# Attention scores from block-diagonal float32 query tiles of 64 queries, and a new table of priorities, in an attention and two-layer kernel on one core

## The chip, the core and the metric

The kernel runs on one core of one Trainium2 chip. The metric is device time in microseconds (us) for one execution. A core has five engines with instruction queues of their own, each worked off in order: PE (TensorE, matrix products), DVE (VectorE), ACT (ScalarE), POOL (GpSimd) and SP (SyncE, which here issues every DMA). The weight loads of PE have a row of their own, PEld. Sixteen DMA engines carry out the transfers that SP issues.

## The reference

There are four batches, eight heads, 576 positions and 64 elements to a head. Attention is causal by blocks of 64 positions: a query sees all keys of its own block and of the blocks before it. Two layers with 2048 hidden units follow on the 2304 x 512 result.

```python
batch, n_heads, seq, head_dim = (4, 8, 576, 64)
scores = scale * np.matmul(q, k.transpose(0, 1, 3, 2))
mask = pos[:, None] // 64 >= pos[None, :] // 64
scores = np.where(mask, scores, -1000000000.0)
attn = np.exp(scores - np.max(scores, axis=-1, keepdims=True))
attn = attn / (np.sum(attn, axis=-1, keepdims=True) + 1e-09)
x = np.matmul(attn, v)                 # then heads side by side: 2304 x 512
h = x @ w_in;  g = np.maximum(h, 0) + alpha * np.minimum(h, 0);  x = g @ w_out
h = x @ w_in2; g = h / (1 + np.exp(-1.702 * h));                 out = g @ w_out2
```

Weights of the layers come as float64 bits and are narrowed in the kernel.

## The kernel before

**Passes.** A pass handles one pair of heads of one batch. Batch 0 is cut into eight half passes, first queries 0 to 319 of the four pairs (group 0), then queries 320 to 575 (group 1); the other three batches are twelve whole passes.

**One pass.** SP loads q, k and v of the pair in rows of one position (256 bytes), q twice, so that it stands twice side by side (`load`). PE transposes them (`prep_t`, tile `tp`). `prep_out` splits the float32 values into a high fp32r part (ACT) and the rest (DVE): of k, the high part lies on 64 partitions and the rest on the other 64; of q there are two tiles, high and rest. `score` multiplies the five query tiles of `QT` (64, 128, 128, 128 and 128 queries against 64, 192, 320, 448 and 576 keys), for each head alone, high q and then rest q against the k tile. A tile of 128 queries holds two blocks, so for the first of them the last 64 keys are overwritten with a large number (the memset in `soft`) before the row minimum (DVE) and the exponential with its sum (ACT). `high` writes the normalized weights as float16 (ACT), `rest` what is missing to it (DVE), into the tile `hl` of one head. A DMA transpose then turns each `hl` of 12 (group 0) or 18 (group 1) chunks of 128 columns into `pt`, of which there are two buffers. `pv` multiplies `pt` with v, which is held as three bf16 parts, and `pv_out` stores the result to `xs`.

**Around it.** While attention runs, PE also computes a first part of layer 0 (the block products, lines 206 and 250 to 252, tiles `h` and `x`), 384 products of 288 columns for each batch, as soon as that batch's attention is done. `warm` products fill PE at the start. After the last pass the pools are swapped, and the rest of both layers follows (lines 744 and 819).

**Order.** Each step is entered with `at(kind, n, fn)`. Its priority is n + 0.1 ORDER + SHIFT of its kind; `arrange` then fixes an order for each engine with its own costs and writes it into the program. `SHIFT` is a table of numbers for each kind of step.

Of the kernel before, what the change touches and what calls it, by code (L numbers as in the profile page):

```python
# [23 lines left out]
QT = [(0, 64, 64, 1, 0), (64, 128, 192, 2, 2), (192, 128, 320, 3, 6), (320, 128, 448, 4, 0), (448, 128, 576, 5, 8)]  # L24

GRP = [((0, 1, 2), 0, 320, 12), ((3, 4), 320, 256, 18)]


PV = [[
    [(0, 64, 0, 0, (0,)), (64, 256, 0, 0, (1, 2)), (128, 64, 1, 64, (1,)), (192, 128, 1, 0, (2,)), (256, 64, 2, 64, (2,))],  # L30
    [(0, 256, 0, 0, (3, 4)), (0, 256, 1, 0, (3, 4)), (0, 256, 2, 0, (3, 4)), (64, 64, 3, 64, (3,)), (128, 128, 3, 0, (4,)),
     (192, 64, 4, 64, (4,))],
], [
    [(0, 64, 0, 0, (0,)), (64, 256, 0, 0, (1, 2)), (64, 256, 1, 0, (1, 2)), (192, 128, 2, 0, (2,))],
    [(0, 256, 0, 0, (3, 4)), (0, 256, 1, 0, (3, 4)), (0, 256, 2, 0, (3, 4)), (0, 256, 3, 0, (3, 4)), (128, 128, 4, 0, (4,))],
]]

SLOT = [((0, 1), (2,)), ((3,), (4,))]
# [10 lines left out]
    "comb 2": 35.0, "comb 3": -62.2, "first": 58.5, "gate": -35.3, "gate 2": 49.1, "gemm1": 46.5,  # L49
    "gemm1 2": 12.5, "gemm2": 59.1, "half": 110.6, "half out": -22.5, "high": 19.0, "load alpha": -0.4,  # L50
    "load k": 9.7, "load q": -168.0, "load v": -25.2, "load w": 61.9, "load w 2": 11.9, "load w 3": 3.0,
    "load wc": -24.2, "load x": -20.5, "narrow": 297.4, "narrow 2": 65.6, "narrow 3": 20.9, "norm": 13.4,
    "out": 4.8, "prep out": 20.2, "prep t": -7.1, "prep v": 81.6, "pv": 5.9, "pv out": 23.1, "rest": 20.2,
    "score": -5.4, "second": 58.6, "setup": -9.8, "snap": -57.0, "soft": -4.0, "split g": 64.1,
    "split g 2": -56.1, "split w": -8.4, "split w 2": 13.3, "split w 3": -3.0, "split x": 56.6,
    "split x 2": 192.1, "sums": -166.0, "warm": 67.8,
# [5 lines left out]
def kernel(  # L62
# [208 lines left out]
    def plan_x(i, n_split):  # L271
# [7 lines left out]
        for c in range(KD):  # L279
# [11 lines left out]
    nat = {"q": one.tile([128, 9, 2, D], F32, name="nat_q"), "k": one.tile([128, 10, D], F32, name="nat_k"),  # L291
           "v": one.tile([128, 9, D], F32, name="nat_v")}
    vp = [one.tile([128, 9, 4, D], BF16, name=f"vp{i}") for i in range(2)]
    hl = [[one.tile([128, 128 * g[3]], F16, name=f"hl{j}{x}") for x in range(NHL[j])] for j, g in enumerate(GRP)]
    stats = [one.tile([128, 3, 6], F32, name=f"stat{j}") for j in range(4)]

    def hl_part(j, x, m, n, h):
        o = 128 * (QT[j][4] + x * QT[j][3])
        return hl[0 if j < 3 else 1][h][0:m, o + 64 * h:o + 64 * h + n]


    def setup():
        pool.memset(ident, 0.0)
        pool.affine_select(out=ident, in_=ident, pattern=[[-1, 128]], compare_op=ALU.not_equal,
                           fill=1.0, base=0, channel_multiplier=1)
        pool.memset(mk_l, 0.0)
        pool.memset(nat["k"][:, 9], 0.0)
        for t in vp:
            pool.memset(t[:, :, 3], 0.0)
        for t in hl[0] + hl[1]:  # L310
            dve.memset(t, 0.0)
        for t in stats:
            pool.memset(t, 1.0)
# [7 lines left out]
    def load(i, nm):  # L321
        b, p, gs = passes[i]
        src = {"q": q, "k": k, "v": v}[nm][b, 2 * p:2 * p + 2].rearrange("h t d -> (h t) d").rearrange("(c p) d -> p c d", p=128)
        if nm == "q":
            c = slice(0, 9) if len(gs) == 2 else (slice(0, 7), slice(2, 9))[gs[0]]
            for y in range(2):
                sp.dma_start(out=nat["q"][:, c, y], in_=src[:, c])
        elif nm == "v" or gs[0] == 0:
            c = slice(0, 9 if nm == "k" or gs[-1] == 1 else 7)
            sp.dma_start(out=nat[nm][:, c], in_=src[:, c])  # L330


    CH = ((0, 1, 2, 3), (4, 5, 6, 7)), ((0, 1, 2), (4, 5, 6)), ((2, 3, 4), (7, 8))

    def chunks(i, what):
        gs = passes[i][2]
        return CH[0 if len(gs) == 2 else 1 + gs[0]][int(what[1])]

    def prep_t(i, what):
        ps = ps_a.tile([128, 512], F32, tag="tv", bufs=2, name="tp")  # L340
        st["tp", i, what] = ps
        if what == "k":

            ts = [nat["k"][:, c:c + 2] for c in range(0, 8, 2)]
        elif what == "tail":
            ts = [nat["k"][:, 8:10]] + [nat["q"][:, 8]] * (len(passes[i][2]) == 2)
        else:
            ts = [nat["q"][:, c] for c in chunks(i, what)]
        for z, t in enumerate(ts):
            pe.transpose(ps[:, 128 * z:128 * z + 128], t.rearrange("p c d -> p (c d)"), ident)  # L350

    def prep_out(i, what):


        ps = st.pop(("tp", i, what))
        gs = passes[i][2]
        if what in ("k", "tail"):
            if i < N0:

                p = passes[i][1]  # L360
                if what == "k" and p == 0:
                    st["k0"] = blk.tile([128, KD, S], F32R, tag="xl0", name="k0")
                if what == "k":
                    st["k0", p] = st["k0"][:, 2 * p:2 * p + 2] if p < KD // 2 else two.tile([128, 2, S], F32R, tag="k", name="k0")
                z = st["k0", p]
            else:
                if what == "k":
                    st[i, "k"] = two.tile([128, 2, S], F32R, tag="k", name="ks")
                z = st[i, "k"]
            z = z.rearrange("p h t -> p (h t)").rearrange("p (c t) -> p c t", t=128)  # L370
            half = [slice(0, 64), slice(64, 128)]
            y = ps.rearrange("p (c t) -> p c t", t=128)
            if what == "k":
                kinds = [(x, y[half[x]], slice(x, 8, 2)) for x in range(2)]
            else:
                kinds = [(0, y[half[0], 0:1], slice(8, 9))]
# [4 lines left out]
        if what == "k" or what == "tail" and len(gs) == 1:  # L381
            return
        if (i, "q") not in st:
            st[i, "q"] = two.tile([128, 2, 2 * S], F32R, tag="q", name="qs")
        if what == "tail":
            c0, y = 8, ps[:, 128:256]
        else:
            cs = chunks(i, what)
            c0, y = cs[0], ps[:, 0:128 * len(cs)]
        t = slice(128 * c0, 128 * c0 + y.shape[-1])  # L390
        z = st[i, "q"]
        hi_part(z[:, 0, t], y, -scale)
# [12 lines left out]
    for i, (b, p, gs) in enumerate(passes):  # L405
        first.append(2 * len(slots))
        for g in gs:
            for s in range(2):
                slots.append((i, g, s))
# [735 lines left out]
```

## Time and profile before

| | |
|---|---|
| median of 3 runs | 1064.5 us (1062.02 to 1065.96) |
| profiled execution | 1065.77 us |
| its span, first to last instruction | 1064.0 us |
| PE, DVE, ACT, POOL busy | 994.3, 739.2, 614.7, 368.0 us |
| mean granted clock of PE | 0.980 of full |
| DMA | 308081 packets, 216.92 MB |

The profiled execution is one of the program on the chip. Its span leaves 1.77 us outside. Busy times are sums over one engine's instructions in the span; engines work beside one another, so they don't add up to it. The ends of matrix products are modelled, so PE counts as busy for a little longer than it takes columns in.

### The profile page before, as it was taken

To read this page: it belongs to the slowest core of one execution; us is meant where nothing else is said; L and a number is where in the kernel's file an instruction comes from. 1 tells how busy PE (TensorE), PEld (TensorE's weight loads), DVE (VectorE), ACT (ScalarE), POOL (GpSimd) and SP (SyncE) were. 2 spreads that over 40 slices of the span, in tenths; PEclk is the share of its full clock that TensorE was granted. 3 is DMA by queue.
4 is the path that set the end of the run, shared out by engine and by line. 5 is a ranking of instruction groups with operands and counts; after the bars stand their busy time and mean duration, and the time that the engine had idled before them with its cause. 6 is when DMAs were issued, how large, how long until landed. Compare 5 with 4: busy or idle time off the path is not lost.

```text
span 1064.0 us, 19650 instructions
## 1 busy us (share of the span) xinstructions
PE 994.3 (93%) x6934; PEld 892.6 (84%) x6934; DVE 739.2 (69%) x1434; ACT 614.7 (58%) x1492; POOL 368.0 (35%) x385
## 2 busy tenths in 40 slices
PE   6776888999999999899999998989999999999998
PEld 4454778889888989899989897878888999999897
DVE  7868998898988985768886877778843544443422
ACT  6777888988888984455554545445542443342332
POOL 3334352535242442665453543423331311111100
PEclk8889899999999999999999999999999999999999
DMA  7999989998999977675556487988675666574360
GB/s 185 190 195 201 210 175 222 212 221 196 220 207 217 207 164 194 225 254 175 194 178 218 159 288 239 317 273 270 226 241 165 233 194 195 176 243 130 119 198 30
DMA packets 308081, 216.92 MB, mean 204 GB/s; under 512 B 219664, under 2 KB 246288, under 8 KB 307984
## 3 DMA queue, kind: packets, MB, share of 16 engines
q1 hardware_dynamic: 307984, 215.67, 74.4%
q8 instruction: 55, 0.90, 0.4%
q14 instruction: 42, 0.34, 0.1%
HBM read 143.27 MB, written 40.89 MB: 173 GB/s over the span
## 4 chain that ended last, share of the span: by engine, by line
PE 57%; DMA 7%; ACT 3%; DVE 3%; issue 3%; POOL 1%; SPq 0%; ACTq 0%; DVEq 0%; POOLq 0%
PE acc L819 24%; PE ga L744 13%; PE ep L744 9%; PE h L206 4%; DMA rw<-in_moe_w_out_dram 2%; PE pv L524 2%; DMA pt<-hl 2%; PE x L251 1%; PE x L250 1%; PE x L252 1%; DMA wc<-wc 1%; DMA xa<-xo 1%; DMA o<-xa 1%; DMA x2s<-o 1%; PE sc L446 1%
## 5 line engine op out<-in xcount | busy, mean ns | idle before, releaser
L819 PE MATMUL acc<-wh,gs 128*128 128x512 f32 x576 | 186.1, 391 | 4.3 <-ACT wh L124 2.5
L744 PE MATMUL ga<-xc,ws 128*128 128x256 f32 x1368 | 184.4, 283 | 0.2
L744 PEld LDWEIGHTS ga<-xc,ws 128*128 128x128 f32 x1368 | 176.8, 192 | 5.9 <-DVE gs L127 0.8
L744 PE MATMUL ep<-xc,ws 128*128 128x256 f32 x936 | 131.8, 283 | 2.6 <-DVE gs L127 2.6
L819 PEld LDWEIGHTS acc<-wh,gs 128*128 128x128 f32 x576 | 108.1, 188 | 27.4 <-ACT wh L124 2.7
L744 PEld LDWEIGHTS ep<-xc,ws 128*128 128x128 f32 x936 | 121.1, 192 | 4.0 <-DVE gs L127 3.6
L770 POOL TENSOR_TENSOR v<-u,v 128x256 f32<-128x256 f32 x48 | 38.6, 805 | 214.3 <-ACT v L769 214.3
L819 PE MATMUL acc<-wl,gs 128*128 128x512 f32 x288 | 112.6, 391 | 0.0
L768 ACT ACTIVATE u<-ga 128x512 f32<-128x512 f32 x48 | 28.5, 593 | 139.3 <-PE ga L744 139.2
L524 PE MATMUL pv<-pt,vp 128*128 128x256 f16 (+2 forms) x960 | 90.9, 242 | 12.6 <-DMA pt<-hl 11.0
L819 PE MATMUL acc<-gs,wh 128*128 128x512 f32 (+1 forms) x320 | 92.5, 373 | 4.0 <-DVE o L829 4.0
L499 DVE SCALAR_TENSOR_TENSOR hl<-e,stat,hl 64x64 f16<-64x64 f32 (+4 forms) x160 | 90.7, 605 | 4.6 <-ACT hl L489 4.1
L792 DVE TENSOR_TENSOR u<-ep,v 128x256 f32<-128x256 f32 x48 | 20.2, 421 | 101.8 <-PE ep L744 101.8
L127 POOL TENSOR_TENSOR gs<-g,gs 128x288 fp32r<-128x288 f32 x64 | 61.2, 963 | 83.6 <-ACT gs L124 77.3
L206 PE MATMUL h<-xh,wh 128*128 128x288 f32 x256 | 79.3, 310 | 8.5 <-DVE g L221 3.6
L489 ACT ACTIVATE hl<-e,stat 64x64 f16<-64x64 f32 (+4 forms) x160 | 79.4, 553 | 12.2 <-issue 6.1
L524 PEld LDWEIGHTS <-vp 128*128 128x128 bf16 x960 | 63.3, 99 | 27.4 <-DMA pt<-hl 9.6
L469 ACT ACTIVATE e<-sc,stat 64x64 f32<-64x64 f32 (+4 forms) x160 | 82.7, 519 | 2.4 <-DVE stat L461 1.3
L206 PE MATMUL h<-xlb,wh 128*128 128x288 f32 x256 | 78.1, 305 | 0.1
L206 PE MATMUL h<-xh,wl 128*128 128x288 f32 x256 | 77.2, 302 | 0.0
L250 PE MATMUL x<-gs,wh 128*128 128x288 f32 x256 | 75.8, 301 | 1.0 <-DVE g L221 0.4
L252 PE MATMUL x<-gs,wl 128*128 128x288 f32 x256 | 75.8, 298 | 0.0
(98 smaller groups left out, 2313.1 us busy)
## 6 DMA issues: line engine op xcount, KB each, us to landing
ws<-wc SPq DMA_DIRECT2D x284, 256.0 KB, 3.9
wc<-wc SPq DMA_DIRECT2D x84, 256.0 KB, 2.8
rw<-in_moe_w_in_dram SPq DMA_DIRECT2D x32, 512.0 KB, 4.5
rw<-in_moe_w_out_dram SPq DMA_DIRECT2D x32, 512.0 KB, 4.0
nat_q<-in_q_dram SPq DMA_DIRECT2D x24, 288.0 KB, 4.0
nat_k<-in_k_dram SPq DMA_DIRECT2D x16, 288.0 KB, 4.4
nat_v<-in_v_dram SPq DMA_DIRECT2D x16, 288.0 KB, 4.1
xa<-xo SPq DMA_DIRECT2D x32, 144.0 KB, 3.3
```

The source lines that it names most:

```text
L127: eng.tensor_tensor(out=dst, in0=src, in1=hi.bitcast(F32), op=ALU.subtract)
L206: pe.matmul(ps, st_[:, sl], mv[:, c], start=z == 0, stop=z == 3 * KD - 1)
L250: pe.matmul(ps, oh[:, sl], gh, start=f == 0, stop=False)
L252: pe.matmul(ps, ol[:, sl], gh, start=False, stop=f == NA - 1)
L469: act.activation(out=eo, in_=v[:, h] if len(heads) > 1 else v, func=ACTF.Exp, scale=-1.0, bias=stat[0:m, 0, a:a + 1], accum_out=stat[0:m, ...
L489: act.activation(out=o, in_=e, func=ACTF.Copy, scale=r)
L499: dve.scalar_tensor_tensor(out=hl_part(j, 1, m, nk, h), in0=es[h][0:m, off:off + nk], scalar=stat[0:m, 2, 2 * a + h:2 * a + h + 1], in1=hl ...
L524: pe.matmul(o, l, r, start=z == 0, stop=z == len(ops) - 1)
L744: pe.matmul(ps, st_, mv, start=first and z == 0, stop=last and z == 5, skip_group_check=True)
L768: act.activation(out=u, in_=g, func=ACTF.Copy)
L770: pool.tensor_tensor(out=v, in0=u[:, TH:TB], in1=v, op=ALU.subtract)
L819: pe.matmul(ps, a, b_, start=first and z == 0, stop=last and z == 2)
```

## The change

The scores are formed from nine blocks of 64 queries in place of five tiles. For each block the stationary tile `qd` is block-diagonal: on 64 partitions and 64 columns lies the q of one head, on the other 64 and 64 that of the other head, and zeros (written once at the start) elsewhere. One float32 product of this tile with a k tile that holds both heads gives the scores of 64 queries of both heads on 128 partitions. Neither q nor k is split, no key is masked since a block sees whole blocks of keys, and q is loaded once. q, k and v are loaded head by head, 128 positions to a chunk, with a load of its own for the 64 positions left over. The softmax works in three parts of a pass (blocks 0 to 4, blocks 5 and 6, blocks 7 and 8) with both heads in one tile; there is one `hl` and one DMA transpose for each part (18, 14 and 18 chunks), and `pt` keeps its two buffers. The high part of blocks 7 and 8 moves from ACT to DVE. All numbers of `SHIFT` change.

```diff
-QT = [(0, 64, 64, 1, 0), (64, 128, 192, 2, 2), (192, 128, 320, 3, 6), (320, 128, 448, 4, 0), (448, 128, 576, 5, 8)]
...
+PART = [((4, 2, 3, 1, 0), {1: 0, 0: 1, 2: 2, 3: 4, 4: 6}, 9), ((5, 6), {5: 0, 6: 3}, 7), ((7, 8), {7: 0, 8: 4}, 9)]
...
+STEP = [(((4, 2, 3, 1, 0), 0, 3),), (((5, 6), 1, 2), ((7,), 2, 1.5), ((8,), 2, 1.5))]
...
-    "comb 2": 35.0, "comb 3": -62.2, "first": 58.5, "gate": -35.3, "gate 2": 49.1, "gemm1": 46.5,
...
+    "comb 2": 68.3, "comb 3": -29.8, "first": 33.5, "gate": -46.3, "gate 2": -7.9, "gemm1": 59.5,
...
-            c = slice(0, 9) if len(gs) == 2 else (slice(0, 7), slice(2, 9))[gs[0]]
-            for y in range(2):
-                sp.dma_start(out=nat["q"][:, c, y], in_=src[:, c])
...
+            for h in range(2):
+                sp.dma_start(out=t[:, 0:c, h], in_=src[h, 0:128 * c].rearrange("(c t) d -> t c d", t=128))
+            if m:
+                sp.dma_start(out=t[0:m, c], in_=src[:, 128 * c:128 * c + m].rearrange("h t d -> t h d"))
...
-            for x, s_, c in kinds:
-                hi_part(z[half[x], c], s_)
-            for x, s_, c in kinds:
-                lo_part(dve, z[half[1 - x], c], s_, z[half[x], c])
...
-        hi_part(z[:, 0, t], y, -scale)
-        dve.scalar_tensor_tensor(out=z[:, 1, t], in0=y, scalar=-scale, in1=z[:, 0, t].bitcast(F32), op0=ALU.mult, op1=ALU.subtract)
...
+                dve.tensor_copy(out=st[key][:, 128 * cs[0]:128 * cs[0] + n], in_=ps[:, y:y + n])
...
+                for h in range(2):
+                    x = slice(64 * h, 64 * h + 64)
+                    hi_part(z[x, b0 + 2 * cs[0]:b0 + 2 * cs[0] + n, x], ps[x, y:y + 64 * n].rearrange("p (c t) -> p c t", t=64), -scale)
...
-                for h, (o, k0, n_) in zip(heads, part):
-                    for x in range(2):
-                        pe.matmul(o, qs[:, x, S * h + q0:S * h + q0 + m], ks[:, h, k0:k0 + n_], start=x == 0, stop=x == 1)
...
+            for w, k0, n_ in parts:
+                pe.matmul(w, qs[:, y], ks[:, k0:k0 + n_], start=True, stop=True)
...
-                dve.memset(v[0:64, :, nk - 64:nk] if len(heads) > 1 else v[0:64, 1, nk // 2 - 64:nk // 2], BIG)
...
+            if part == 2:
+                dve.tensor_scalar(out=hl_part(part, y, 0), in0=e, scalar1=stat[:, 2, a:a + 1], scalar2=1.0, op0=ALU.mult, op1=ALU.mult)
+            else:
+                act.activation(out=hl_part(part, y, 0), in_=e, func=ACTF.Copy, scale=stat[:, 2, a:a + 1])
...
+        n = 2 * PART[part][2]
+        pt = two.tile([128, 18, 128], F16, tag="pt", bufs=PTB, name="pt")[:, 0:n]
+        sp.dma_start_transpose(out=pt, in_=hl[part].rearrange("p x c -> p (x c)"))
```

On SP, a stretch inside a whole pass of batch 1, before (`nat_q`, `nat_k` and `nat_v` are loads of q, k and v; `pt<-hl` are DMA transposes; `wc` and `xs` are stores):

```order
L503 DMA_TRANSPOSE pt<-hl_183 128x18x128
L654 DMA wc_0_2_80<-wc 128x512
L503 DMA_TRANSPOSE pt<-hl_180 128x12x128
L654 DMA wc_0_1_79<-wc 128x512
L539 DMA xs<-x 128x256
L327 DMA nat_q<-in_q_dram 128x9x64
L330 DMA nat_k<-in_k_dram 128x9x64
L503 DMA_TRANSPOSE pt<-hl_181 128x12x128
L327 DMA nat_q<-in_q_dram 128x9x64
L654 DMA wc_0_3_81<-wc 128x512
L503 DMA_TRANSPOSE pt<-hl_182 128x18x128
L654 DMA wc_0_4_82<-wc 128x512
```

The same queue now, inside a whole pass of batch 2:

```order
L337 DMA nat_k<-in_k_dram 128x4x64
L339 DMA nat_k<-in_k_dram 64x2x64
L337 DMA nat_v<-in_v_dram 128x4x64
L339 DMA nat_v<-in_v_dram 64x2x64
L466 DMA_TRANSPOSE pt<-hl_184 128x18x128
L337 DMA nat_k<-in_k_dram 128x4x64
L337 DMA nat_v<-in_v_dram 128x4x64
L611 DMA wc_1_1_86<-wc 128x512
L611 DMA wc_1_2_87<-wc 128x512
L330 DMA nat_q<-in_q_dram 128x4x64
L332 DMA nat_q<-in_q_dram 64x2x64
L466 DMA_TRANSPOSE pt<-hl_182 128x18x128
```

A pass had four loads of up to 1152 rows and four transposes; it has nine smaller loads and three transposes, each of which carries both heads.

On PE, the scores of group 0 of one whole pass before (`ks` is the k tile, `qs` the split q; x4 stands for two heads, high and rest), among block products:

```order
L446 MATMUL sc_2099<-ks_1884,qs_1963 64x64 x4
L446 MATMUL sc_2099<-ks_1884,qs_1963 128x192 x4
L251 MATMUL x2_1908<-gs_163,wh1_1180 128x288
L446 MATMUL sc_2189<-ks_1884,qs_1963 128x320 x4
L252 MATMUL x2_1908<-gs_163,wl1_1181 128x288
```

The same scores of one whole pass now, between a block product and the products with v:

```order
L203 MATMUL h_2163<-xh_1752,wl0_814 128x288
L421 MATMUL sc_2310<-ks_2078,qd1_181 128x320
L421 MATMUL sc_2310<-ks_2078,qd1_181 128x192
L421 MATMUL sc_2310<-ks_2078,qd1_181 128x256
L421 MATMUL sc_2310<-ks_2078,qd1_181 128x128
L421 MATMUL sc_2310<-ks_2078,qd1_181 128x64
L480 LDWEIGHTS vp1_179
L480 MATMUL pv_2135<-pt_2082,vp1_179 128x128
```

Twelve products in two score tiles became five products in one, and both heads arrive together.

## Rows read from the trace of the kernel before

**Rows 1.** SP's timeline around three moments: start, us, what it issued.

```profile
24.90 1.39 SPq L503 DMA_TRANSPOSE pt<-hl  x1
...
145.84 0.97 SPq L539 DMA_DIRECT2D xs<-x  x1
...
418.14 0.32 SPq L539 DMA_DIRECT2D xs<-x  x1
```

**Rows 2.** Windows: stretch, its us, busy us (instructions) by engine, PEclk, DMA share, GB/s.

```profile
0.00:146.00 146.00, 111.01 (x774) 83.16 (x775) 117.71 (x240) 109.48 (x279) 61.66 (x63) 0.89 0.91 192
146.00:236.00 90.00, 80.95 (x671) 73.95 (x670) 79.54 (x166) 75.42 (x211) 32.27 (x33) 0.98 1.02 219
236.00:331.00 95.00, 90.45 (x769) 83.90 (x767) 81.03 (x176) 82.18 (x232) 36.74 (x41) 1.00 0.97 204
331.00:418.00 87.00, 83.87 (x714) 78.45 (x713) 66.09 (x141) 67.22 (x189) 34.29 (x36) 1.00 0.85 185
418.00:480.00 62.00, 59.15 (x437) 58.53 (x436) 44.24 (x63) 33.74 (x78) 39.93 (x37) 0.97 0.75 246
480.00:1064.00 584.00, 568.89 (x3580) 514.62 (x3578) 350.59 (x653) 246.63 (x510) 163.13 (x178) 1.00 0.62 203
```

**Rows 3.** DMA queues, window 0 to 146, then window 480 to 1064.

```profile
DMA packets 80168, 28.07 MB, mean 192 GB/s; under 512 B 73627, under 2 KB 79131, under 8 KB 80155
q1 hardware_dynamic: 80155, 27.91, 90.4%
...
DMA packets 66135, 118.39 MB, mean 203 GB/s; under 512 B 6495, under 2 KB 14815, under 8 KB 66087
q1 hardware_dynamic: 66087, 117.76, 61.1%
```

**Rows 4.** Chain that ended last, inside 277 to 300, 410 to 470, 484 to 500.

```profile
280.36 6.58 DMA pt<-hl
297.35 7.68 DMA pt<-hl
...
417.24 11.08 PE h L206 x83
...
484.69 5.47 PE acc L819 x24
```

**Rows 5.** PE's timeline, 299 to 312.

```profile
305.44 0.61 PE L350 MATMUL tp<-ident,nat_q 128*128 128x128 f32 x4
307.48 0.90 PE L446 MATMUL sc<-ks,qs 128*64 128x64 f32 x8
309.93 0.93 PE L524 MATMUL pv<-pt,vp 128*128 128x256 f16 x15
```

**Rows 6.** Groups by form, 0 to 480: busy us, mean ns, idle before.

```profile
L350 PE MATMUL tp<-ident,nat_q 128*128 128x128 f32 x152 | 27.3, 293 | 11.4 <-DMA nat_q<-in_q_dram 4.6 <-DVE stat L461 3.0 <-DVE sq L160 2.5
...
L127 DVE TENSOR_TENSOR ks<-tp,ks 64x512 fp32r<-64x512 f32 x24 | 16.5, 689 | 0.7
L393 DVE SCALAR_TENSOR_TENSOR qs<-tp,qs 128x512 fp32r<-128x512 f32 x24 | 16.4, 681 | 2.2 <-ACT qs L124 1.9
L489 ACT ACTIVATE hl<-e,stat 128x320 f16<-128x320 f32 x32 | 17.6, 551 | 0.0
L124 ACT ACTIVATE ks<-tp 64x512 fp32r<-64x512 f32 x24 | 14.1, 589 | 4.2 <-PE tp L350 4.0
L124 ACT ACTIVATE qs<-tp 128x512 fp32r<-128x512 f32 x24 | 14.0, 589 | 6.6 <-PE tp L350 6.6
```

**Rows 7.** SP's timeline, 286 to 298: start, us for the issue.

```profile
286.52 4.22 SPq L503 DMA_TRANSPOSE pt<-hl  x1
...
291.40 0.43 SPq L327 DMA_DIRECT2D nat_q<-in_q_dram  x1
292.00 3.49 SPq L503 DMA_TRANSPOSE pt<-hl  x1
```

**Rows 8.** The page's groups: the products with v.

```profile
L524 PE MATMUL pv<-pt,vp 128*128 128x256 f16 (+2 forms) x960 | 90.9, 242 | 12.6 <-DMA pt<-hl 11.0
```

More of the change, by code (lines that the diff above doesn't have):

```diff
@@ new lines, in todo_, with prep_t @@
+    def todo_(i):
+        gs = passes[i][2]
+        kq = [("k", c) for c in range(5)]
+        qs = [("q", c) for c in range(5)]
+        if len(gs) == 2:
+            return kq[:4], kq[4:] + qs[:3], qs[3:]
+        return (kq[:4], kq[4:] + qs[:3]) if gs[0] == 0 else (qs[:2],)
+    def prep_t(i, z):
+        ps = ps_a.tile([128, 512], F32, tag="tv", bufs=2, name="tp")
+        st["tp", i, z] = ps
+        for y, (nm, c) in enumerate(todo_(i)[z]):
+            t = nat[nm][:, c]
+            pe.transpose(ps[:, 128 * y:128 * y + 128], t.rearrange("p h d -> p (h d)"), ident)
@@ L436, in score @@
-    def score(n):
-        i, g, s = slots[n]
+            for blocks_, part, length in STEP[g]:
+                slots.append((i, g, blocks_, part))
+                place_.append(n)
+                n += length
+    first.append(n)
+    NS = n
+    def score(u):
+        i, g, bs, part = slots[u]
         qs = st[i, "q"]
         ks = st["k0", passes[i][1]] if i < N0 else st[i, "k"]
-        st[n, "sc"] = views(n)
-        for j, off, heads, parts, _ in st[n, "sc"]:
-            q0, m, nk, ch, c0 = QT[j]
-            for part in parts:
-                for h, (o, k0, n_) in zip(heads, part):
-                    for x in range(2):
-                        pe.matmul(o, qs[:, x, S * h + q0:S * h + q0 + m], ks[:, h, k0:k0 + n_], start=x == 0, stop=x == 1)
@@ new lines, in score, with soft @@
+        st[u, "sc"] = vs
+    count = [0]
+    def soft(u):
+        i, g, bs, part = slots[u]
+        if bs[0] == PART[part][0][0]:
+            st["stat", i, part] = stats[count[0] % 4], []
+            count[0] += 1
+        stat, es = st["stat", i, part]
+        e = two.tile([128, 960], F32, tag="e", bufs=2, name="e") if len(bs) > 1 else two.tile([128, S], F32, tag="f", bufs=2, name="e")
+        vs, new, o = st.pop((u, "sc")), [], 0
+        for y, v in vs:
+            a = PART[part][0].index(y)
+            dve.tensor_reduce(out=stat[:, 0, a:a + 1], in_=v, op=ALU.min, axis=AX.X if y < 8 else AX.XY)
+            new.append((a, y, e[:, o:o + 64 * (y + 1)]))
+            o += 64 * (y + 1)
+        for (y, v), (a, _, eo) in zip(vs, new):
+            act.activation(out=eo if y < 8 else eo.rearrange("p (a b) -> p a b", a=2), in_=v, func=ACTF.Exp, scale=-1.0,
+                           bias=stat[:, 0, a:a + 1], accum_out=stat[:, 1, a:a + 1])
+        es += new
```

288 lines of the change are left out of this document (110 added, 178 removed).

## The prediction

> **What bounds the kernel now.** I read the windows by stage first, then the DMA queues, then SP's timeline. The stores of `xs` mark the stages: batch 0's last one is issued at 145.84, the last of all at 418.14 [rows 1]. In the first stage, 0 to 146, PE is busy for 111 us only, some of it with warm products, and no compute engine is full (DVE 81%, ACT 75%), but the DMA engines are at 0.91 [rows 2]. From 146 to 331 they stand at 1.02 and 0.97, with PE busy at 90% and 95%. From 331 to 418 their share falls to 0.85 while PE is at 96%. After 480 PE is busy for 568.9 of 584 us [rows 2]. So the transfers set the pace first, then transfers and PE together, then PE alone. From 146 on PE's work counts: of the 334 us to 480 the four windows show it busy for 314.4, idle for 19.6.
>
> Small packets fill the DMA engines. 73627 of 80168 packets before 146 are under 512 bytes [rows 3]. They come from the 256-byte rows of q, k and v and from the transposes. Their price follows from two stretches, one of mostly small packets, one of mostly large ones. 0.904 x 146 us x 16 engines = 2112 us went to 73627 small and 6541 larger packets; 0.611 x 584 x 16 = 5709 us to 6495 small and 59640 larger [rows 2, 3]. Two equations give 20.4 ns for a small packet. Were all packets before 146 alike, it would be 26.3 ns.
>
> **The change, part by part.**
>
> Transfers. For one pair of heads of batch 0, q was loaded twice in both half passes (4 x 896 rows), k once (1152), v in 896 and 1152 rows: 6784. Now it is 1152 + 1152 + 1920 = 4224. The transposes fall from 60 chunks of 128 rows to 50, so by 1280 packets. Four pairs lose 4 x (2560 + 1280) = 15360 packets, and 15360 x 20.4 ns / 16 = 19.6 us of all sixteen engines (25 at 26.3 ns). A whole pass loses 1152 + 1280 = 2432 packets, 3.1 us of its 22.7 (272 us from 146 to 418, over twelve passes).
>
> SP's own time. A pass has nine loads for four, at 0.4 us or so each [rows 7], so 2 us more. A transpose took 1.39 us to issue at the start and 3.5 to 4.2 in a crowded stretch [rows 1, 7], so some 12 us for the four of a pass; they carry a sixth less, about 2 us. I count SP at nothing.
>
> ACT, for a whole pass. `high` falls from ten instructions to seven, of 64 to 448 columns, with 0.55 us for the middle one [rows 6]: about 2.0 us less. The copies of k (two of 0.59 us and a small one) go, those of q shrink: about 1.3 less. One exponential fewer is 0.7. In sum about 4 us of some 20. DVE loses the rests of k and q (four instructions of 0.68 us and two small ones: 3.3 us) and the memsets (0.7), has one `rest` instruction and two tenths of its columns less (1.0), and gains copies of k (1.0) and the high parts of blocks 7 and 8 (1.3): about 2.5 us less. I count neither as time, since neither bounds a stage; they shorten waits.
>
> PE. A product of 512 columns takes 5.47 / 24 = 0.228 us, one of 288 takes 11.08 / 83 = 0.1335 [rows 4], so a column costs 0.42 ns and an instruction 12 ns. Scores before: 6400 columns in 24 products, 2.99 us a pass. Now there are 2880 columns in 10 products, but in float32, which this trace shows for transposes alone. There, four of 128 columns span 0.61 us, the last 0.29 of it its own length, so 0.107 us each, two steps for a column [rows 5, 6]. That is the low end: 2.55 us. The kernel before builds an exact product out of four partial ones (high and rest of q with high and rest of k), and gets two of them at once because they lie on the two halves of the partitions. The new tile fills both halves with heads, so I take four steps: 11520 x 0.42 + 0.1 = 5.0 us, or 2.0 more. The high end is eight steps, 9.8 us.
>
> The Trainium skill (TensorE: Matmul & The Clock Gate, section Terms) says that transpose mode makes float32 four times faster. By that a score column would take four times a transposed one, eight steps, and the scores 9.8 us a pass in place of my 5.0. The trace has no float32 product other than transposes, so it can't decide; I return to eight steps below as a rival worked out from rows.
>
> The four tall-and-short products of 64 queries go with their changes of tile height: the eight products around them span 0.90 us [rows 5], where 1024 columns, eight instructions and a tail of 0.19 make 0.72, so 0.2 less. Four transposes fewer: 0.4 less. `pv` falls from 10368 to 9600 columns, 0.3 less, and rises from 60 to 78 instructions; fifteen of them with 1728 columns took 0.93 us [rows 5], which leaves next to nothing for an instruction, at most 12 ns: I take 0.2 less. In sum PE has 2.0 - 0.2 - 0.4 - 0.2 = 1.2 us more in each pass.
>
> The first stage. Transfers bound it, so it should lose most of 19.6 us. Against that, the first transpose stands behind seven loads of weights in SP's order where it stood behind four; three of half a megabyte at about 190 GB/s are 8 us, most of which later stages of the same 146 us get back. PE's 4 x 1.2 us are hidden by its 35 idle us, and would be added if these were gone. The zeros for `qd` go to POOL, busy for 62 of 146. I take 17 less; bounds 8 and 25.
>
> From 146 to 480. PE gains 12 x 1.2 = 14.4 us. If its 19.6 idle us stay, the stage is 14.4 longer. If idle time falls to the share of the last stage (15.1 of 584, 2.6%), it lasts (314.4 + 14.4) / 0.974 = 337.6, or 3.6 longer. DVE, ACT and the DMA engines all lose an eighth or more, so I take 5.
>
> From 480 on nothing changes but the priorities: 0, within 4 either way.
>
> Sum: -17 + 5 = -12 against the profiled execution's 1065.77 us, 1053.8. That execution is 1.3 us above the median of the three runs, so the forecast is **1053 us**.
>
> **The rivals.**
>
> *PE takes it all back.* The first stage gives only 8 us, since its passes are held by chains of waits and not by packets, and the 14.4 us of PE come in full: +6, or nothing that can be measured. For it: all windows to 418 show several engines at 80 to 95%. Against it: the DMA share of 0.91 and 1.02. Time 1059 to 1071.
>
> *A float32 product of eight steps.* Scores cost 9.85 - 2.99 = 6.9 us more a pass, and PE 6.1 more in all. Twelve passes are 73, less 19 by filled idle time and transfers, and the first stage still gives 8: about 1110. It turns from faster to slower at about five steps: a step is 2880 x 0.42 = 1.2 us a pass, 14.5 us in twelve. For it the rule named above, against it the four partial products.
>
> *Two buffers for three transposes.* This one ends slower by other means. A transpose now holds both heads, its buffer is free only when both heads' products are done, and two buffers serve three transposes. One round of a pass is two landings and two pairs of products: 2 x 7.1 us [rows 4] + 2 x 1.4 + 2 x 0.9 + two waits of about 1.6 us behind block products, 22.1 us, beside 22.7 now. Should a landing take 8 us, since group 0's transpose grows from 12 to 18 chunks, a pass takes 24: 15 us more in twelve passes. PE's order leaves 97 block products more (13 us) behind the last pass than before, so these aren't filled in, and the total is 1065.8 - 17 + 15 + 13 = 1077. Against it: the order lets `pv` read part 1's transpose for both heads before it waits for part 2's. It decides from landings of about 7.3 us on.
>
> *More than forecast.* Two steps for a float32 column, or a first stage bound by packets alone (-25): 1030 to 1040.
>
> **How the numbers follow.** The forecast, 1040 to 1059, has 0.55; more than that 0.08; PE takes it back 0.17; two buffers, or another new wait, 0.15; eight steps 0.05. The range 1034 to 1073 leaves out the larger part of the last two and a tail of the fastest, 2 in 10. A measurement of this kernel can't tell 0.5% (5.3 us) from no change: faster than 1059 has 0.63, between 0.17, slower 0.20.
>
> **What would show it.** Right: the eighth store of `xs` at 120 to 138 in place of 145.84; about 80000 - 15000 small packets up to the same store in the program; a DMA share under 0.9 between the eighth store and the 24th; 10 score products of a pass in about 5 us, a 512-column one near 0.86 us; PE idle for 12 us or less over the 334. Wrong: a 512-column score product at 0.43 or 1.7 us; products with v that wait for `pt<-hl` more than the 11.0 us of now [rows 8]; the eighth store still near 146 with DMA at 0.8, which would mean that a chain of waits and not packets held the first stage; or a last stage other than 584 us, which would be the priorities.

## The result and the profile after

| | before | after |
|---|---|---|
| median | 1064.96 us (1062.02 to 1065.96, 4 runs) | 1053.56 us (1050.43 to 1056.34, 4 runs) |
| profiled execution, its span | 1065.77, 1064.0 us | 1056.34, 1054.6 us |
| PE, DVE, ACT, POOL busy | 994.3, 739.2, 614.7, 368.0 us | 1003.4, 708.7, 570.6, 369.5 us |
| PE idle in the span | 69.7 us | 51.2 us |
| DMA packets | 308081 | 264370 |

The ratio is 0.9897, with an interval of 0.9858 to 0.9936: faster by 1.0%, where 1053 us was forecast. PE has 9.1 us more to do and waits 18.5 us less, which are the 9.4 us between the two profiled executions.

SP's timeline of the changed kernel: the first transpose, and the stores of `xs` that end batch 0 (the eighth) and the last pass (the 32nd). They answer to [rows 1].

```profile
28.94 3.40 SPq L466 DMA_TRANSPOSE pt<-hl  x1
...
134.99 0.54 SPq L495 DMA_DIRECT2D xs<-x  x1
...
398.29 0.33 SPq L495 DMA_DIRECT2D xs<-x  x1
```

The windows by stage, with the columns of [rows 2]; cut at the 8th, 16th, 24th and 32nd store.

```profile
0.00:135.00 135.00, 108.50 (x767) 78.57 (x768) 107.28 (x216) 91.37 (x234) 58.80 (x62) 0.94 0.77 173
135.00:221.40 86.40, 82.46 (x713) 71.83 (x712) 72.95 (x160) 66.96 (x188) 36.83 (x37) 1.00 0.85 193
221.40:314.30 92.90, 88.85 (x750) 78.60 (x748) 72.09 (x164) 70.90 (x208) 35.26 (x38) 0.98 0.85 187
314.30:398.30 84.00, 82.95 (x756) 77.16 (x756) 58.02 (x127) 56.24 (x155) 34.23 (x38) 1.00 0.74 164
398.30:470.50 72.20, 68.19 (x506) 66.53 (x505) 46.32 (x68) 36.04 (x83) 42.11 (x42) 1.00 0.69 226
470.50:1054.50 584.00, 572.42 (x3604) 519.11 (x3602) 352.06 (x648) 249.09 (x510) 162.28 (x176) 0.99 0.61 202
```

The eighth store comes 10.9 us sooner. The stretch from there to 470.5 takes 335.5 us, where 334 were read before, and the last one 584.0 as before. So the whole gain lies ahead of the eighth store. The DMA engines, which stood at 0.91, 1.02 and 0.97, are at 0.77, 0.85 and 0.85. PE's granted clock rose from 0.89 to 0.94 in the first stage; that is not what moved the store, since two variants of the changed kernel from below, `after_still` and `after_sp`, had 0.91 and 0.95 there with their eighth stores 0.6 us apart:

```profile
0.00:136.00 136.00, 108.33 (x758) 77.96 (x758) 106.74 (x213) 90.44 (x234) 60.16 (x62) 0.91 0.79 171
...
0.00:135.40 135.40, 106.96 (x767) 76.74 (x768) 107.08 (x216) 91.53 (x234) 60.14 (x62) 0.95 0.77 173
```

The DMA queues up to the eighth store, to be held against the first two lines of [rows 3]: 17869 small packets fewer.

```profile
DMA packets 62298, 23.38 MB, mean 173 GB/s; under 512 B 55758, under 2 KB 61262, under 8 KB 62286
...
q1 hardware_dynamic: 62286, 23.23, 76.3%
```

PE's timeline of the changed kernel inside 300 to 322: score products. Each is recorded as two MATMULs, so x10 are five products, x2 is one.

```profile
301.77 1.88 PE L421 MATMUL sc<-ks,qd 128*128 128x320 f32 x10
...
304.03 0.86 PE L421 MATMUL sc<-ks,qd 128*128 128x384 f32 x2
...
312.15 1.02 PE L421 MATMUL sc<-ks,qd 128*128 128x448 f32 x2
...
314.34 1.12 PE L421 MATMUL sc<-ks,qd 128*128 128x512 f32 x2
```

From 384 to 448 columns a product grows by 0.16 us, 2.5 ns a column with the scatter of a single look; the five products of part 0 have 960 columns and span 1.88 us, of which 0.19 are the tail that the prediction read from [rows 5]. That is 1.76 ns a column, four steps of 0.42 ns and some overhead.

PE's groups by line, of the kernel before from 146 to 480 and then of the changed one from 135 to 474: products with v and scores.

```profile
L524 PE MATMUL pv<-pt,vp 128*128 128x256 f16 (+1 forms) x705 | 64.8, 241 | 8.3 <-DMA pt<-hl 7.5 <-DVE qs L393 0.4 <-DVE wa L159 0.4
L446 PE MATMUL sc<-ks,qs 128*128 128x288 f32 (+4 forms) x252 | 48.4, 315 | 1.7 <-ACT e L469 1.3
```

```profile
L480 PE MATMUL pv<-pt,vp 128*128 128x128 f16 (+3 forms) x936 | 61.1, 218 | 2.3 <-DMA pt<-hl 2.3
L421 PE MATMUL sc<-ks,qd 128*128 128x512 f32 (+4 forms) x206 | 61.0, 423 | 1.8 <-ACT qd L121 1.0 <-ACT e L441 0.5
```

The scores cost 12.6 us more, the products with v 3.7 less, and PE waits for a transpose for 2.3 us in place of 7.5. Over the whole span it waits for transposes about as long as in [rows 8], most of it in the first stage:

```profile
L480 PE MATMUL pv<-pt,vp 128*128 128x128 f16 (+3 forms) x1248 | 83.4, 220 | 12.7 <-DMA pt<-hl 12.6
```

Where PE's ledger hides a shift: up to the 32nd store the twelve passes take 263.3 us where they took 272.3, but from there to the first `acc` product 76.3 us pass where 66.4 did. Windows from the eighth store to the 32nd and on to the first `acc`, of the kernel before and then of the changed one:

```profile
145.84:418.10 272.26, 255.53 (x2152) 236.57 (x2152) 226.92 (x481) 225.09 (x629) 103.47 (x109) 0.99 0.95 203
418.10:484.50 66.40, 63.55 (x473) 62.93 (x472) 47.82 (x69) 35.73 (x82) 43.92 (x40) 0.97 0.76 252
```

```profile
135.00:398.30 263.30, 254.25 (x2216) 227.59 (x2215) 203.07 (x450) 194.10 (x550) 106.31 (x111) 0.99 0.82 182
398.30:474.60 76.30, 72.29 (x538) 70.49 (x537) 48.83 (x72) 39.44 (x90) 44.65 (x44) 1.00 0.71 235
```

PE has 65 instructions more behind the last pass (538 for 473): block products that the new order leaves for later. The passes' 9 us are a shift of work, not a gain.

### The profile page after: what moved, and what is told of

It reads as the page before. It is cut to its first block, busy times and chain, and to the rows that moved or that the text cites. A ratio compares the mean times of both kernels' runs of the same rounds, so it can differ in the third digit from the quotient of the medians.

```text
span 1054.6 us, 19799 instructions
## 1 busy us (share of the span) xinstructions
PE 1003.4 (95%) x7086; PEld 891.8 (85%) x7086; DVE 708.7 (67%) x1381; ACT 570.6 (54%) x1376; POOL 369.5 (35%) x389
## 2 busy tenths in 40 slices
DMA packets 264370, 205.53 MB, mean 195 GB/s; under 512 B 175952, under 2 KB 202576, under 8 KB 264272
## 5 line engine op out<-in xcount | busy, mean ns | idle before, releaser
L480 PEld LDWEIGHTS <-vp 128*128 128x128 bf16 x1248 | 73.9, 99 | 26.8 <-DMA pt<-hl 10.8
L776 PE MATMUL acc<-gs,wh 128*128 128x512 f32 (+1 forms) x320 | 92.8, 375 | 3.6 <-DVE o L786 3.6
L480 PE MATMUL pv<-pt,vp 128*128 128x128 f16 (+3 forms) x1248 | 83.4, 220 | 12.7 <-DMA pt<-hl 12.6
L124 POOL TENSOR_TENSOR gs<-g,gs 128x288 fp32r<-128x288 f32 x64 | 56.3, 882 | 88.4 <-ACT gs L121 67.0
L462 DVE SCALAR_TENSOR_TENSOR hl<-e,stat,hl 128x448 f16<-128x448 f32 (+8 forms) x144 | 85.0, 636 | 3.1 <-ACT hl L457 2.6
L441 ACT ACTIVATE e<-sc,stat 128x320 f32<-128x320 f32 (+8 forms) x144 | 74.7, 524 | 11.9 <-DVE stat L437 8.4
L247 PE MATMUL x<-gs,wh 128*128 128x288 f32 x256 | 78.0, 310 | 3.0 <-DVE g L218 2.1
L248 PE MATMUL x<-gs,wh 128*128 128x288 f32 x256 | 76.1, 299 | 0.6 <-POOL gs L124 0.6
```

What stands on the lines that cost most here:

```text
L124: eng.tensor_tensor(out=dst, in0=src, in1=hi.bitcast(F32), op=ALU.subtract)
L247: pe.matmul(ps, oh[:, sl], gh, start=f == 0, stop=False)
L248: pe.matmul(ps, oh[:, sl], gl, start=False, stop=False)
L441: act.activation(out=eo if y < 8 else eo.rearrange("p (a b) -> p a b", a=2), in_=v, func=ACTF.Exp, scale=-1.0, bias=stat[:, 0, a:a + 1], a ...
L462: dve.scalar_tensor_tensor(out=hl_part(part, y, 1), in0=e, scalar=stat[:, 2, a:a + 1], in1=hl_part(part, y, 0), op0=ALU.mult, op1=ALU.subt ...
L480: pe.matmul(o, l, r, start=z == 0, stop=z == len(ops) - 1)
```

## The experiments

All landmarks are from one profiled execution each, read from SP's and PE's timelines: the eighth store of `xs`, the stretch from there to the 32nd, from there to the first `acc` product, and the rest of the span. Kernels with the same order and the same work agree in them to some 3 us, in the last stretch to 6. A profiled execution can also lie off its kernel's median: that of `after_sp` took 1071.91 us, that of `after_q2` 1072.59.

| kernel | median | 8th store | to 32nd | to `acc` | rest |
|---|---|---|---|---|---|
| before | 1064.96 | 145.8 | 272.3 | 66.4 | 579.4 |
| after | 1053.56 | 135.0 | 263.3 | 76.3 | 580.0 |
| before, q copied once (`before_q1`) | 1057.39 | 142.5 | 269.1 | 66.4 | 575.2 |
| after, q loaded twice, early (`after_q2`) | 1077.77 | 158.5 | 262.7 | 75.2 | 574.3 |
| after, q loaded twice, spread (`after_q2b`) | 1066.05 | 139.2 | 272.5 | 74.8 | 574.6 |
| after, one-step scores (`after_fp32r`) | 1055.46 | 135.4 | 264.4 | 77.1 | 578.2 |
| after, three `pt` (`after_pt3`) | 1054.64 | 135.6 | 265.1 | 76.5 | 574.7 |
| after, no product waits for `pt` (`after_still`) | 1058.00 | 136.0 | 269.0 | 75.3 | 576.3 |
| after, light softmax (`after_light`) | 1052.31 | 132.8 | 262.2 | 75.9 | 578.2 |
| after, light softmax, one-step scores | 1043.11 | 131.0 | 258.8 | 76.4 | 574.3 |
| after, 144 tiny loads (`after_sp`) | 1064.79 | 135.4 | 279.5 | 76.1 | 579.0 |
| after, one-step scores, planned so | 1052.42 | 128.6 | 259.1 | 64.4 | 599.4 |
| after, old priorities | 1087.02 | 137.4 | 245.8 | 114.7 | 587.3 |
| before, new priorities | 1104.35 | 153.4 | 295.1 | 65.4 | 592.5 |

The kernel before ran beside them in three groups, with medians of 1063.60, 1063.66 and 1061.78 us; every ratio below is to the runs of its own group.

### Packets

**The kernel before with the second copy of q cut to one chunk**, 18 loads of 20, in the same order.

```diff
-            for y in range(2):
-                sp.dma_start(out=nat["q"][:, c, y], in_=src[:, c])
+            sp.dma_start(out=nat["q"][:, c, 0], in_=src[:, c])
+            if i in (0, 4):
+                sp.dma_start(out=nat["q"][:, c, 1], in_=src[:, c])
+            else:
+                sp.dma_start(out=nat["q"][:, c.start:c.start + 1, 1], in_=src[:, c.start:c.start + 1])
```

> The kernel before, with the second copy of q cut to one chunk of 128 rows in 18 of its 20 loads; the scores then use rows of an earlier pass in that copy, so values change but no instruction and no order. 6 x 768 packets go in batch 0 (5.9 us of all DMA engines at 20.4 ns) and 12 x 1024 later (15.7 us). Theory packets (the small packets set the pace of the first stage): eighth store of xs 4 to 7 us earlier than 145.84, attention's last store 8 to 15 us earlier, total 4 to 13 us less. Rival waits (chains of waits and buffers set the pace, a full DMA queue is only its company): eighth store and total within 3 us.

Ratio 0.9943 (0.992 to 0.9966), 1057.39 us. Up to the eighth store (a window cut at it) it moved 73297 packets for 79986, which at the prediction's 20.4 ns / 16 are 8.5 us of the DMA engines, and the store came 3.3 us sooner. In the passes it moved 10207 packets fewer (13.0 us) and gained 3.2. So with DMA at 0.91 and above, a packet saved gave back 0.39 and 0.25 of its price. Each of these two landmarks is no larger than their scatter; the medians of the runs differ by 6.2 us, clear of noise, which is 0.29 of the 21.5 us.

**The changed kernel with q loaded a second time**, into a tile that nobody reads; the planner put these loads as early as it could.

```diff
+    twice = one.tile([128, 9, D], F32, name="twice")
...
+            w = slice(0, 9) if len(gs) == 2 else (slice(0, 7), slice(2, 9))[gs[0]]
+            again = q[b, 2 * p:2 * p + 2].rearrange("h t d -> (h t) d").rearrange("(c p) d -> p c d", p=128)
+            sp.dma_start(out=twice[:, w], in_=again[:, w])
```

> The changed kernel, with a second load of q of the old kind beside each first one, into a tile that nothing reads; all other instructions in the same order. Adds 8 x 896 packets in batch 0 (9.1 us of all DMA engines at 20.4 ns) and 12 x 1152 later (17.6 us). Theory packets: eighth store of xs 6 to 9 us later than 134.99, total 6 to 12 us more, since PE waits later. Rival waits (at a DMA share of 0.77 there is room): eighth store and total within 3 us.

Ratio 1.0119 (1.0092 to 1.0146), 1077.77 us. It did not test what it was meant to: 18 of the 20 loads were issued before 75 us. Nearly all of the 20992 packets (26.8 us) fell into the first stage, whose end moved by 23.5 us; after it nothing is lost. Nor are the 23.5 us a price of packets: all these loads write the same tile, so such a load can't be issued before the one before it has landed, and everything behind it on SP waits with it. SP's longest wait up to 75 us (total, times, longest):

```profile
SPq L336 <- DMA twice<-in_q_dram: 16.1, 12, 2.4
```

If all of that came through, 7.4 us were left for the packets, 0.28 of their price (an estimate).

**The same loads, each placed right behind its sibling** by one more dependency for the planner.

```diff
+            if a.tensor.name.startswith('twice'):
+                c = (-70, 0, 0)
+                need.add(k - 1)
```

> The changed kernel with q loaded a second time (into a tile that nobody reads), each second load right behind its sibling on the queue, so that the added packets are spread over the passes as in the kernel before: 1152 more of 256 bytes in each whole pass, 640 or 512 in each half pass of batch 0. Packets set the pace everywhere: 6 us by batch 0's last store of xs (4 x 1152 packets at 20.4 ns / 16), 1.5 us in each of the twelve whole passes, 24 us in all. Latency through the in-order queues sets it from about 75 us on (our theory now): 3 us by the fourth store, 3 to 6 by the eighth, and at most 4 more for the twelve whole passes, so 4 to 8 us in all. Packets count for nothing: within 2 us at every landmark.

Ratio 1.0028 (0.9998 to 1.0058), 1066.05 us. The DMA queues of this kernel up to its eighth store, at 139.2:

```profile
DMA packets 71913, 25.80 MB, mean 185 GB/s; under 512 B 65373, under 2 KB 70877, under 8 KB 71901
```

9615 packets more than in the changed kernel (12.3 us, since loads for the next passes are among them) cost at most 4.2 us here, 0.34 of their price. One of the added loads waited for the landing of the one before it again, from 84.7 to 88.2:

```profile
SPq L336 <- DMA twice<-in_q_dram: 3.5, 1, 3.5
```

2.7 of the 4.2 us came up around it, between the fourth store (75.8 for 74.5 in the changed kernel) and the fifth (92.8 for 88.8). In the passes, where no load waited so, 11697 more (14.9 us), with ten issues on SP, cost 9.2. Neither theory had it: more than latency alone, less than packets alone. The second load of q, spread as the work is and with its 20 issues, costs 12.5 us of the total (1066.05 less 1053.56), about as much as the whole change gained.

### PE and the transposes

**One-step scores.** `qd` and the k tile are rounded to fp32r, whose products take one step a column; the planner is told the old cost, so the order stays.

```diff
-    qd = [one.tile([128, 9, 128], F32, name=f"qd{i}") for i in range(2)]
+    qd = [one.tile([128, 9, 128], F32R, name=f"qd{i}") for i in range(2)]
...
-                    st[key] = st["k0"][:, p] if i < N0 else two.tile([128, S], F32, tag="k", name="ks")
+                    st[key] = st["k0"][:, p] if i < N0 else two.tile([128, S], F32R, tag="k", name="ks")
...
+        one_ = mv.dtype == F32R and 'sc_' in outs[0].tensor.name
+        cols, load = free_size(outs[0]) * (4 if one_ else 1 if mv.dtype != F32 else 2 if turn else 4), free_size(w)
```

> The changed kernel, with q and k of the scores held as fp32r, so that a score column takes one step and not four (the scores lose precision); same instructions in the same order. 8640 column steps of 0.42 ns are 3.6 us a pass, 43 us in the twelve passes after batch 0. Theory PE (PE alone sets the pace from 135 to 470): that stage 30 to 43 us shorter, first stage within 3 us, total 30 to 43 us less. Rival shared (DVE, ACT and transfers stand close behind PE): 8 to 20 us less.

Ratio 0.9921 (0.9893 to 0.995), 1055.46 us: no gain. A 512-column score product is now a single record, from PE's timeline; then the window of the twelve passes:

```profile
299.44 0.39 PE L421 MATMUL sc<-ks,qd 128*128 128x512 f32 x1
```

```profile
135.40:399.80 264.40, 229.67 (x2108) 212.78 (x2108) 204.84 (x450) 193.51 (x550) 109.62 (x111) 0.97 0.85 181
```

PE is busy for 24.6 us less in the passes (254.25 before) and they last 1.1 us longer. A PE at 97% did not set the pace. (PE's granted clock there was 0.97, for 0.99 in the changed kernel; its busy time already holds that.) Its waits in that window:

```profile
PE pv L480 <- DMA pt<-hl: 9.5, 8, 2.1
PE sc L421 <- ACT e L441: 6.9, 11, 1.2
PE sc L421 <- ACT qd L121: 4.6, 3, 3.6
PE x L247 <- DVE g L218: 3.1, 1, 3.1
```

What PE was freed from, it now waits for, spread over the transposes and what ACT and DVE hand it.

**Three buffers for `pt`**, order unchanged.

```diff
-    PTB = 2
+    PTB = 3
```

> The changed kernel, with three buffers for the transposed weights in place of two, in the same order. Theory buffers (in the first stage the transposes wait until both heads' products with v have read a buffer: SP's wait for them is 7.7 us there): eighth store of xs 4 to 8 us earlier than 134.99, total 4 to 10 us less. Rival (the transposes would wait for DVE's weights just after, or packets are short): within 2 us.

Ratio 0.9915 (0.9894 to 0.9936), 1054.64 us: the rival of two buffers for three transposes falls. It needed landings of 7.3 us or more; in the passes of the changed kernel a transpose landed 4.9 us after its issue (median of 35, 3.9 to 7.3).

**No product waits for a transpose.** The products with v read a tile of zeros.

```diff
+    still = one.tile([128, 18, 128], F16, name="still")
...
-                mv = pt[:, z:z + step * (n // 64 - 1) + 1:step, 64 * h:64 * h + 64]
+                mv = still[:, z:z + step * (n // 64 - 1) + 1:step, 64 * h:64 * h + 64]
```

> The changed kernel with the products of v reading a fixed tile of zeros in place of the transposed probabilities; the transposes still run and still wait for their tiles, but no product waits for a landing, and the attention part of the output is zero. The landings' latency in the loop of transpose, products with v, copy and addition sets the pace of a pass (our theory): the interval from the fourth to the eighth store of xs falls from 60 us to under 52, a whole pass from 21.9 us to 20.5 or less. The engines' own work or SP's issues set it: both intervals stay within 5% (57 to 63, 20.8 to 23). A zero product may also let TensorE's granted clock or power behave differently, so only the intervals and the waits are read, not the last stage.

Ratio 0.9938 (0.9915 to 0.9962), 1058.00 us. The passes take 269.0 us, not fewer but 5.7 more; the interval from the fourth to the eighth store is 60.0 us (76.0 to 136.0), where the changed kernel has 60.5. The theory of landings, which I had formed after the first runs, falls as well. The granted clock was 0.985 over the whole span, for 0.986 in the changed kernel. Why the passes are a little longer stays open.

**Lighter softmax.** Minimum, exponential, high and rest take 64 columns of each block.

```diff
-            dve.tensor_reduce(out=stat[:, 0, a:a + 1], in_=v, op=ALU.min, axis=AX.X if y < 8 else AX.XY)
+            dve.tensor_reduce(out=stat[:, 0, a:a + 1], in_=v[:, 0:64] if y < 8 else v[:, 0, 0:64], op=ALU.min, axis=AX.X)
...
-                act.activation(out=hl_part(part, y, 0), in_=e, func=ACTF.Copy, scale=stat[:, 2, a:a + 1])
+                act.activation(out=hl_part(part, y, 0)[:, 0:64], in_=e[:, 0:64], func=ACTF.Copy, scale=stat[:, 2, a:a + 1])
```

> The changed kernel with lighter work between a score product and its transpose: minimum, exponential, high and rest of every block read and write 64 columns only, so all probabilities but the first 64 of a block are zero or left over (the attention part of the output is not the reference's). Instructions, their order, the loads and the transposes stay. ACT has some 4 to 5 us less in a whole pass, DVE about 5. If these two engines set the pace of a pass (a theory that the run with cheaper scores leaves): a whole pass falls from 21.9 us to 20 or less, and the 24 stores from the eighth on from 263 us to under 245. If PE sets it, or the queue of SP, or the packets: 258 to 268. If PE and the two share it, each filling what the other leaves: a few us, 250 to 258.

Ratio 0.9909 (0.9878 to 0.994), 1052.31 us, about that of the changed kernel.

**Lighter softmax and one-step scores together**, by the two edits above, with the order unchanged.

> The same lighter work and the score products in one step a column as well, so PE, ACT and DVE all have less in each pass, in the same order (same parts of the output left out). PE and the two others share the pace: the 24 stores from the eighth on take under 240 us, clearly less than in either run by itself. The pace is SP's queue or the transfers: 255 to 268 in this run too.

Ratio 0.9819 (0.9792 to 0.9846), 1043.11 us. The windows of the passes, of the light kernel and then of this one:

```profile
132.80:395.00 262.20, 251.30 (x2215) 226.91 (x2214) 142.58 (x450) 164.28 (x550) 101.83 (x110) 0.99 0.83 183
```

```profile
131.00:389.80 258.80, 226.23 (x2112) 212.61 (x2111) 146.65 (x450) 163.65 (x550) 103.08 (x111) 0.97 0.85 185
```

DVE lost 60.5 and 56.4 us, ACT 30, PE 28 in the second, and the passes 1.1 and 4.5 us of 263. Of the 14.1 us between its span and that of the changed kernel (1040.5 and 1054.6; the medians are 10.45 apart), 4.0 lie ahead of the eighth store, 4.5 in the passes and 5.7 in the last stretch, where its work is the same. Neither PE nor DVE and ACT alone set the pace of a pass, and the three together gave back 4.5 us there of the 28 to 56 that they lost.

### SP's queue

**Nine tiny loads more in a pass**, three of 16 bytes behind each transpose.

```diff
         sp.dma_start_transpose(out=pt, in_=hl[part].rearrange("p x c -> p (x c)"))
+        for _ in range(3):
+            sp.dma_start(out=tiny[:, 4 * cnt_[0]:4 * cnt_[0] + 4], in_=q[0, 0, 0:1, 0:4])
+            cnt_[0] += 1
```

> The changed kernel with nine loads of 16 bytes more on SP's queue in a whole pass (three behind each transpose, 144 in all, into a tile that nobody reads): nine issues of about 0.4 us, 3.9 us of SP's time a pass, and no transfer to speak of; the order of all else is the same. If SP's issues set the pace: 2 to 4 us more a pass, 24 to 45 us over the twelve whole passes and 10 or more up to the eighth store. If they don't: the eighth store within 2 us of 135, the passes within 6 us of 263.

Ratio 1.0025 (1.0 to 1.005), 1064.79 us. The passes grow by 16.2 us to 279.5, more than by any other edit that keeps the order, and the first stage, with 36 of the loads, by 0.4. The view of the added loads in the passes (count, then ns min, median and max), the window's row, and the changed kernel's transposes:

```profile
L470 SPq DMA_DIRECT2D tiny<-in_q_dram x108: 223/278/839, 137.1 to 408.8; - x108
```

```profile
135.40:414.90 279.50, 260.60 (x2215) 231.04 (x2214) 202.97 (x450) 194.36 (x550) 107.10 (x111) 0.97 0.79 171
```

```profile
L466 SPq DMA_TRANSPOSE pt<-hl x35: 1297/2764/4582, 136.7 to 385.7; - x35
```

The 108 issues sum to 33.9 us, and each is followed by about 0.1 us before the next starts, so SP has 45 us more to do. 16 of them show: some 0.36 us for each us, less than the 2 to 4 us a pass of the theory, far more than nothing. The share is uncertain: the medians of the two kernels differ by 11.2 us (0.25), and in this execution PE's granted clock was 0.97 in the passes for 0.99, with PE busy 6.4 us longer for the same work, so a part may be the clock's. The transfers are no more (DMA 0.79 for 0.82). In the changed kernel SP's 205 DMA issues in the passes sum to 189 us of 263, or some 210 with a pause for each; 96.5 of them are 35 transposes. With the added loads it is 252 of 279.5.

### The order

**Old priorities in the new kernel, new priorities in the old one.** Only the table `SHIFT` is exchanged, for instance:

```diff
-    "rest": 10.2, "score": -51.1, "second": 33.6, "setup": 41.6, "snap": 67.5, "soft": 19.4, "split g": -13.8,
...
+    "out": 4.8, "prep out": 20.2, "prep t": -7.1, "prep v": 81.6, "pv": 5.9, "pv out": 23.1, "rest": 20.2,
```

> The changed kernel with the table of priorities of the kernel before: structure without priorities. If the structure (fewer loads and chunks, float32 scores, three transposes) brings the gain: within 6 us of the changed kernel, eighth store of xs within 5 us of its 135. If the new table brings it: near 1064 us, eighth store near 146. A table that was fitted to another structure may also cost more than either: then the two can't be added, and the total is above 1070.

> The kernel before with the changed kernel's table of priorities: priorities without structure. If the structure brings the gain: within 6 us of the kernel before (1058 to 1070), eighth store of xs at 143 to 150. If the table brings it: near 1054 us, with the eighth store near 135. If the table only fits the new structure: over 1070.

Ratios 1.0227 (1.019 to 1.0265) and 1.0378 (1.0341 to 1.0414): each is slower than both kernels. The new structure under the old table, from the first window to the last:

```profile
0.00:137.40 137.40, 113.29 (x801) 81.17 (x802) 106.33 (x215) 91.25 (x243) 60.21 (x63) 0.93 0.74 164
137.40:383.20 245.80, 226.52 (x1964) 197.55 (x1963) 199.86 (x433) 178.04 (x504) 93.60 (x90) 0.97 0.83 182
383.20:497.90 114.70, 106.47 (x774) 102.16 (x773) 69.18 (x101) 57.48 (x137) 68.52 (x71) 1.00 0.67 215
497.90:1085.20 587.30, 568.52 (x3553) 515.07 (x3552) 348.05 (x635) 241.75 (x494) 159.25 (x167) 0.98 0.59 193
```

The eighth store is still 8.4 us sooner than before, so most of the first stage's gain is the structure's. But only 1964 PE instructions stand in the passes, for 2216, and 774 behind them, for 538: the passes are 17.5 us shorter, the stretch behind them 38.4 us longer, and PE is idle for 70 us in all, as before the change, for 51. SP had about as much to issue in these shorter passes, 190 issues of 185 us, with its transposes about as long as in the changed kernel (median 2.91 us for 2.76):

```profile
L466 SPq DMA_TRANSPOSE pt<-hl x34: 1331/2908/4522, 138.0 to 374.1; - x34
```

So SP's own load fits into 245.8 us, and it alone did not make the passes of the changed kernel 263 us long. The table and the structure don't add up: 1064 with neither, 1054 with both, 1087 and 1104 with one.

**One-step scores, with the planner told of their cost**, so that the order changes: the two lines on `one_` are taken back.

```diff
-        one_ = mv.dtype == F32R and 'sc_' in outs[0].tensor.name
```

> The changed kernel with score products of one step a column, and the planner told of it, so that the order of the work changes: block products may stand where the shorter scores leave PE free. If what held the run with cheaper scores was the old order, which has no work to put there: 10 to 30 us less than the changed kernel, 1025 to 1045. If the pace of a pass comes from elsewhere than PE: 1045 to 1060. A priority table that was fitted to other costs may lose what it wins: over 1060.

Ratio 0.9902 (0.9878 to 0.9926), 1052.42 us: the same as the changed kernel by its interval. The first `acc` product starts at 452.1, 22.5 us sooner, and the rest then takes 599.4 us for 580.0. PE's longest wait in that rest:

```profile
PE acc L776 <- ACT wh L121: 12.8, 1, 12.8
```

```profile
452.10:1051.50 599.40, 570.83 (x3566) 515.03 (x3564) 360.14 (x656) 251.26 (x512) 164.46 (x180) 0.99 0.61 199
```

With another order the freed PE time is used up to `acc`; later PE waits for weights that are prepared too late, 28.6 us idle for 11.7. No version that keeps the whole computation beat the changed kernel clear of noise.

## Why the prediction was right, and where it was not

**The total** came out 0.6 us from the forecast, the sign and the place (ahead of the eighth store) as forecast. Two terms missed and nearly made up for one another: -17 was -10.9, and +5 was +1.5. The forecast sum of -12 was -9.4 between the two profiled executions and -11.4 between the medians. So that the number is so close is in part luck.

**The first stage.** The packets went as said, even more of them (17869 small ones for the 15360 counted, since transposes and loads also moved behind the store). The step that was mis-sized is the one that took nearly the whole price of a packet as time: "Transfers bound it, so it should lose most of 19.6 us". Cut at the stores themselves the difference is 17688 packets (79986 and 62298); at 20.4 ns / 16 they are 22.6 us, and 10.9 came, 0.48. The runs on q give 0.39 (a saving) and at most 0.34 (an addition) up to the eighth store. At 0.39 the packets would be worth 8.8 of the 10.9 us; that they make up most of the gain is supported by these runs, and what made the rest stays open. A DMA share of 0.91 did not mean that every packet less shortened the stage. The first transpose was issued 4.0 us later (28.94 for 24.90), with six loads of weights ahead of it in SP's timeline for four, and that was made good by the fourth store, at 74.5 for 83.2.

**From 146 to 480.** The step "From 146 on PE's work counts" is wrong, though its number was near. 24.6 us less for PE gave nothing, with the same order. The PE count itself was mis-sized too: 14.4 us more were forecast, and from the eighth store to the first `acc` it is 326.5 for 319.1, 7.5 more. Scores gave 12.6 in place of 21.6 (the 2.0 less 0.2 of twelve passes). Scores run ahead of the stores, so the stretch holds only some ten passes' worth on either side (252 records at 24 a pass, 206 at 20); a pass's scores took 5.9 us for 4.6, so 1.3 more in place of 1.8. The 4.6 stand against 3.0 in the prediction's sum, which counted no tails. Four steps for a float32 column held, so did the lighter products with v (3.7 us for 2.4).

The Trainium skill (TensorE: Matmul & The Clock Gate, section Terms) puts transpose mode at four times the speed of float32. Here a transposed column takes two steps [rows 5, 6] and a float32 score column four, so a factor of two. The rival of eight steps is out.

**SP.** "I count SP at nothing" left out a load that can lengthen a pass. SP's sums in the passes, over all issues in SP's timeline: 46 transposes took 136.6 us and 38 loads of q, k, v 19.8; now 35 take 96.5 and 88 take 55.1. The 2 us a pass on either side were 3 us each, and cancel, as forecast. That a longer queue on SP lengthens a pass is shown from one side, by adding to it. That a shorter one would shorten it was not tried, and the run with the old table speaks against SP as the only cause: about the same load there, and passes of 245.8 us. How much is the transfers' own (the second q cost 9.2 us in the passes, with 6.2 us more of issues and pauses on SP) stays open too. So what paces a pass under the new order is not shown; the runs show only that neither the scores on PE, nor the softmax on DVE and ACT, nor the landings, nor the buffers set it by themselves.

**The priorities.** "From 480 on nothing changes but the priorities: 0" held (584.0). But they can't be parted from the rest of the change: the old table under the new structure costs 33 us.

**What would show it.** Eighth store, DMA share and last stage fell where they were put. The 512-column score product spans 1.12 us, 0.93 without its tail of 0.19, for the 0.86 named. PE's idle time over the middle stretch was 13.1 us, just above the 12 named. One sign of being wrong came up by a little: products with v wait 12.6 us for transposes, for 11.0 before. 10.3 us of that lie ahead of the eighth store, and neither a third buffer nor products that wait for no transpose made the kernel faster.

## What to carry to other kernels

An engine that is busy for 97% of a stretch need not set its pace when the order is fixed: take work from it without changing the order, and see whether the stretch shrinks. A queue that only issues transfers can lengthen the work, so count its issues. An added load is a clean test of packets only if it waits for nothing of its own: loads into one tile wait for one another's landing. A table of priorities belongs to one structure: time a structural change with the order it will run in, and read how many instructions stand in each stretch before calling a shorter stretch a gain.

## What was not expected of the hardware

A float32 product is recorded as two MATMULs, together four steps of 0.42 ns a column, and a fp32r product as one, 0.39 us for 512 columns with its tail. A load of 16 bytes takes SP 0.28 us to issue (median of 108), not much less than the 0.43 us of a load of 1152 rows [rows 7], so on SP it is the number of loads that counts. A transpose holds it for 1.30 to 4.58 us.
